# Loading four operand blocks straight into the place of their low parts, and splitting two of them later in the list

## The chip, the cores and the metric

The kernel runs on one core of a Trainium2 chip. The metric is the device time of one execution in microseconds (us), and less is better. TensorE (PE in the profile) multiplies matrices, with its weight loads shown as PEld; VectorE (DVE) and ScalarE (ACT) do the elementwise work; GpSimd (POOL) and SyncE (SP) mostly issue DMAs here. The rows of SP's DMA queue are marked SPq.

## The reference, cut to what matters

```python
xn = layernorm(x)                                  # x: 1 x 2048 x 640
a = einsum("bsd,ed->bse", xn, dft_hid_re)          # transform along the hidden dimension
b = einsum("bsd,ed->bse", xn, dft_hid_im)
y = einsum("ts,bse->bte", dft_seq_re, a) - einsum("ts,bse->bte", dft_seq_im, b)
gate, up = xn @ W_gate, xn @ W_up                  # 640 x 1728 each
h = (gate * (gate > 0)) * up
return x + y + h @ W_down                          # 1728 x 640
```

Everything is float32, 2048 tokens by 640 channels. Two branches read the same normalised tokens: a Fourier mixing and a gated network.

## The kernel before, in words

**Arithmetic.** A float32 operand is split into a high part, which ScalarE rounds by a copy (L125), and a low part, the source minus the high part, which VectorE makes (L126). `split(hi, lo, src)` issues these two instructions. `mm3` (L128) then runs three matmuls, high by high, high by low and low by high (L131 to L133), of 128 by 128 weights on 512 columns. Matrix products are cut in two in each direction and computed by seven block products in place of eight, which is why the code is full of blocks B11, B12, B21, B22 and of sums T1 to T4 of them.

**Phases.** The first phase normalises the tokens and multiplies them, as weights, with the columns of the sequence transform, streamed from `in_dft` in four chunks of 512 columns. In a chunk every transform block (T10, T11, ... T43 in the list of names) is one unit: a DMA of 128x1024 floats (L690) into a `raw` or `tk` buffer, a sum on VectorE (L686), a split into a `cb` buffer of a ring of three (L722, L723), and 12 or 18 matmuls. The name's first two characters say which of the products, the last digit says which of four groups of tokens. The second phase (`gate_up`, L881) runs over 13 tiles of 128 of the 1728 inner channels, for each half of the tokens. Its operands are the nine blocks of a **set**: the normalised tokens, transposed, as B11, B12, B21, B22, X4 and T1 to T4, 128x1024 floats each. The third phase (`project`, L1094) multiplies the results by the output matrices.

**The first set.** GpSimd's DMAs write its blocks to DRAM during the first phase (L416, L448), from buffers of the pool `stage`, which holds two tiles of 128x1024 floats. During the last chunk of the first phase they come back: `load_set` (L752) gets a `stage` tile for a block, loads the block into it (L760, on SP), and later splits it from there (L764) into the high and low places that `set_parts` (L741) gives. T2, T1, T3 and T4 have their places in a tile `sets_b`, in memory that held the layernorm's tiles (the profile calls it `r`, as digits are left out of names). B11, B21, X4, B12 and B22 have theirs in `xs_early`, the memory of the first half of the tokens, so they can be split only when the last matmuls on that part of the tokens are done. The same two `stage` tiles serve afterwards for the weights of the 64 channels that are left over (L940) and for two loads that the third phase will want (L1041, L1042).

**Order.** `phase` (L789) turns a list of names into units; `drive` (L768) goes through them and issues, at step i, the preparation (sums and splits) of unit i-2, the loads of unit i, and the matmuls of unit i-4. A `K` in the list loads one of T2, T1, T3, T4 (in this order), an `A` loads one of B11, B21, X4, B12, B22, and an `s` splits the block that has waited longest. This gives the program order. It is not the order on the engines: a planner at build time goes by its own costs, takes what is ready on an engine, and prefers what stands earlier in the program. So a load or split that stands late in the list can be put much earlier, into a place where the engine has nothing better. Within one engine, the order it chose is then fixed, and an instruction that waits holds up all behind it. In the second phase the order on PE, DVE and ACT is written by hand (L1072), that of SP and GpSimd is the planner's.

**The passage to the second phase.** The order written by hand begins with the weights of the left-over channels: `rest_weights` splits them (L942), 30 matmuls use them (`gate_up_rest`, L944), and in their shade the first tile's weights are loaded (L845) and split in two halves (L861, L865), with sums in between (L851 to L855). Then comes `gate_up(0)`: the first blocks it takes are B11, B21 and X4, then T1, T2, T4, X4, B22 and T3.

The list of the last chunk before is:

```python
phase(NCHUNK - 1, "T10 T11 T12 T13 T20 K B220 T21 s K B221 T22 s K T23 B222 s K B223 T30 s A T31 A T32 s A T33 s A T40 s A T41 s T42 s T43")
```

Of the kernel before, what the change touches and what calls it, by code (L numbers as in the profile page):

```python
# [7 lines left out]
F32 = mybir.dt.float32  # L8
# [10 lines left out]
NCHUNK = S // CH  # L19
# [40 lines left out]
def fnet_reglu_kernel(  # L60
# [63 lines left out]
    def split(hi, lo, src):  # L124
        nc.scalar.activation(hi, src, AF.Copy)  # L125
        return nc.vector.tensor_tensor(lo, src, hi.bitcast(F32), op=OP.subtract)  # L126
# [342 lines left out]
    def sums_124(g):  # L469


        def make():
            both = lambda g, cs: [xn_block(g, cs, v) for v in range(2)]
            a11, a21, a12, a22 = both(g, K1), both(g, K2), both(g + NH, K1), both(g + NH, K2)
            s1, s2 = (i.rearrange("p (j d) -> p j d", j=SG) for i in (lambda t: (t[:, :CH], t[:, CH:]))(stage()))
            w = s4_part(g)
            tt = nc.vector.tensor_tensor
            f = lambda i: i.bitcast(F32)
            tc.keep_in_program_order(tt(s1, f(a21[0]), f(a22[0]), op=OP.add))
            tt(s1, s1, f(a22[1]), op=OP.add)  # L480
            tt(s2, s1, f(a11[0]), op=OP.subtract)
            tt(s2, s2, f(a11[1]), op=OP.subtract)
            split(*a21, s1)

            tt(s1, f(a12[0]), s2, op=OP.subtract)
            tt(s1, s1, f(a12[1]), op=OP.add)
            split(*a11, s2)
            split(w[:, :, 0], w[:, :, 1], s1)

        todo.append((idle, make, idle, idle))  # L490

    def sums_3(g):


        def make():
            s = stage()[:, :CH].rearrange("p (j d) -> p j d", j=SG)
            tt = nc.vector.tensor_tensor
            a22, s2 = ([xn_block(n, cs, v).bitcast(F32) for v in range(2)] for n, cs in ((g + NH, K2), (g, K1)))
            tc.keep_in_program_order(tt(s, a22[0], s2[0], op=OP.subtract))
            tt(s, s, a22[1], op=OP.add)  # L500
            tt(s, s, s2[1], op=OP.subtract)
            split(xn_block(g + NH, K1, 0), xn_block(g + NH, K1, 1), s)

        todo.append((idle, make, idle, idle))
# [236 lines left out]
    def set_parts(q, i):  # L741
        if i in SETS_A:
            t, b = xs_early, (SETS_A_NEXT, SETS_A)[q].index(i) * 2 * W2
        else:
            t, b = late["sets_b"][q], SETS_B.index(i) * 2 * W2
        return t[:, b : b + W2], t[:, b + W2 : b + 2 * W2]
# [3 lines left out]
        return h[:, j * CH : (j + 1) * CH], l[:, j * CH : (j + 1) * CH]  # L750

    def load_set(q, blocks, get=stage):  # L752
        t = {}

        def load():
            if "sets_b" not in late:
                late["sets_b"] = {1: get_r1(F32R)}
            for i in blocks:
                t[i] = get()
                nc.sync.dma_start(t[i], sets[q][i])  # L760

        def prepare():
            for i in blocks:
                split(*set_parts(q, i), t[i])  # L764

        return load, prepare, idle, idle
# [17 lines left out]
    early_sets, first_sets = list(SETS_A), list(SETS_B)  # L784
# [4 lines left out]
    def phase(c, names):  # L789


        for n in names.split():
            if n == "K":
                later = load_set(1, [first_sets.pop(0)])
                todo.append((later[0], idle, idle, idle))
                splits.append((idle, later[1], idle, idle))
            elif n == "A":
                later = load_set(1, [early_sets.pop(0)])
                todo.append((later[0], idle, idle, idle))
                splits.append((idle, later[1], idle, idle))  # L800
            elif n == "s":
                todo.append(splits.pop(0))
            elif n[0] == "W":
                sums_124(int(n[1]))
            elif n[0] == "V":
                sums_3(int(n[1]))
            elif n[0] == "B" and n[2] == "1":
                first_stream(int(n[3]), n[:3], int(n[4]))
            else:
                stream(c, n[:-1], int(n[-1]))  # L810
            if steps and len(todo) >= SET_UNITS[-len(steps)]:
                token_sets(*steps.pop(0))

    for n in ("B11", "B21"):
        for g in range(NH):
            phase(0, f"{n}0{g} {n}1{g}")
    phase(0, "B1120 B1130 B1121 B1131 W0 B1122 B1132 B1123 W1 B1133 B2120 B2130 W2 B2121 B2131 B2122 V0 W3 B2132 B2123 B2133")
    phase(0, "V1 T10 T11 V2 T12 T13 V3 T20 B220 T21 B221 T22 T23 B222 B223 T30 T31 T32 T33 T40 T41 T42 T43")
    for c in range(1, NCHUNK - 1):
        phase(c, "T10 T11 T12 T13 T20 B220 T21 B221 T22 T23 B222 B223 T30 T31 T32 T33 T40 T41 T42 T43")  # L820
    assert not steps, len(steps)
    phase(NCHUNK - 1, "T10 T11 T12 T13 T20 K B220 T21 s K B221 T22 s K T23 B222 s K B223 T30 s A T31 A T32 s A T33 s A T40 s A T41 s T42 s T43")
    assert not early_sets and not first_sets
    drive(4, 2)
    ph1.close()
# [158 lines left out]
    def next_set(i, n, since=1, get=stage3, soon=False):  # L984

        load, prepare, _, _ = load_set(0, [i], get)

        def first():
            if 0 not in late["sets_b"] and i in SETS_B:
                late["sets_b"][0] = pool("sets").tile([P, len(SETS_B) * 2 * W2], F32R, name="sets_b")  # L990
            load()

        loads[n - since].append(first)
        (urgent if soon else besides)[n].append(prepare)
# [342 lines left out]
```

## Time and profile before

| what | value |
|---|---|
| time, median of 3 runs (range) | 1027.43 us (1026.66 to 1028.2) |
| the profiled execution's own time | 1026.78 us |
| its span, first to last instruction | 1025.0 us |
| mean granted TensorE clock | 0.999 |
| PE busy | 1019.8 us, 4525 matmuls |
| DVE busy | 818.4 us |
| ACT busy | 443.9 us |
| DMA | 236.45 MB, mean 231 GB/s |

The profiled execution lies 0.65 us below the median, inside the range of the three runs. Its own time is 1.78 us above its span. Times inside the trace are counted from the span's start. A row of the timeline gives start, duration, engine, line, operation, tile written and tiles read; in brackets stands how long the engine had stood idle before it, and for whom. The windows give, for stretches of the span, each engine's busy time and its number of instructions. The rows of the waits give the total, the number and the longest.

### The profile page before, as it was taken

To read this page: it belongs to the slowest core of one execution; us is meant where nothing else is said; L and a number is where in the kernel's file an instruction comes from. 1 tells how busy PE (TensorE), PEld (TensorE's weight loads), DVE (VectorE), ACT (ScalarE), POOL (GpSimd) and SP (SyncE) were. 2 spreads that over 40 slices of the span, in tenths; PEclk is the share of its full clock that TensorE was granted. 3 is DMA by queue.
4 is the path that set the end of the run, shared out by engine and by line. 5 is a ranking of instruction groups with operands and counts; after the bars stand their busy time and mean duration, and the time that the engine had idled before them with its cause. 6 is when DMAs were issued, how large, how long until landed. Compare 5 with 4: busy or idle time off the path is not lost.

```text
span 1025.0 us, 12537 instructions
## 1 busy us (share of the span) xinstructions
PE 1019.8 (99%) x4525; PEld 844.5 (82%) x4525; DVE 818.4 (80%) x1113; ACT 443.9 (43%) x571; POOL 96.9 (9%) x161
## 2 busy tenths in 40 slices
PE   9999999999999999999999999999999999999998
PEld 8888888888888888888888888888888888888886
DVE  7967977979989797688878988887586779787776
ACT  6664453333334443333335444443454434553442
POOL 2000010122110001421110000000000001000000
PEclk9999999999999999999999999999999999999999
DMA  8884744966859745873474666654595747994654
GB/s 329 320 284 156 265 152 137 341 245 211 353 195 359 254 169 174 260 239 134 175 249 151 212 239 232 216 219 173 192 354 190 254 147 232 379 334 155 216 172 160
DMA packets 104542, 236.45 MB, mean 231 GB/s; under 512 B 11936, under 2 KB 55328, under 8 KB 102944
## 3 DMA queue, kind: packets, MB, share of 16 engines
q1 hardware_dynamic: 86896, 165.49, 47.6%
q0 software_dynamic: 17152, 69.74, 18.4%
q8 instruction: 35, 0.57, 0.2%
q10 hardware_dynamic: 432, 0.43, 0.1%
q14 instruction: 27, 0.22, 0.1%
HBM read 179.50 MB, written 55.07 MB: 229 GB/s over the span
## 4 chain that ended last, share of the span: by engine, by line
PE 99%; DVE 0%; issue 0%
PE ps L132 32%; PE ps L131 32%; PE ps L133 32%; PE ps L519 3%; PE ps L548 1%; PE ps L1221 1%; PE ps L113 1%; DVE y L1252 0%; DVE warm L109 0%; DVE eps_t L102 0%; DVE half_t L104 0%
## 5 line engine op out<-in xcount | busy, mean ns | idle before, releaser
L133 PE MATMUL ps<-cb,wt 128*128 128x512 f32 x412 | 159.9, 388 | 0.0
L132 PE MATMUL ps<-cb,wt 128*128 128x512 f32 x412 | 159.9, 388 | 0.0
L131 PE MATMUL ps<-cb,wt 128*128 128x512 f32 x412 | 159.9, 388 | 0.0
L126 DVE TENSOR_TENSOR cb<-rw,cb 128x1024 fp32r<-128x1024 f32 x83 | 93.9, 1132 | 51.6 <-ACT cb L125 51.3
L125 ACT ACTIVATE cb<-rw 128x1024 fp32r<-128x1024 f32 x83 | 81.9, 987 | 117.5 <-PE ps L133 103.0
L125 ACT ACTIVATE cb<-raw 128x1024 fp32r<-128x1024 f32 x64 | 67.9, 1061 | 102.5 <-PE ps L133 91.6
L131 PE MATMUL ps<-xs_early,gw 128*128 128x512 f32 x260 | 101.2, 389 | 0.0
L133 PE MATMUL ps<-xs_early,gw 128*128 128x512 f32 x260 | 101.2, 389 | 0.0
L132 PE MATMUL ps<-xs_early,gw 128*128 128x512 f32 x260 | 101.2, 389 | 0.0
L126 DVE TENSOR_TENSOR cb<-raw,cb 128x1024 fp32r<-128x1024 f32 x64 | 78.2, 1221 | 28.7 <-ACT cb L125 28.3
L122 ACT ACTIVATE gw<-z 128x1024 fp32r<-128x1024 f32 (+1 forms) x52 | 57.7, 1110 | 79.7 <-DVE z L855 74.1
L131 PEld LDWEIGHTS ps<-cb,wt 128*128 128x128 f32 x412 | 77.3, 188 | 16.0
L132 PEld LDWEIGHTS ps<-cb,wt 128*128 128x128 f32 x412 | 77.3, 188 | 16.0
L133 PEld LDWEIGHTS ps<-cb,wt 128*128 128x128 f32 x412 | 77.3, 188 | 15.9
L131 PE MATMUL ps<-cb,xs_late 128*128 128x512 f32 x232 | 90.3, 389 | 0.0
L132 PE MATMUL ps<-cb,xs_late 128*128 128x512 f32 x232 | 90.3, 389 | 0.0
L133 PE MATMUL ps<-cb,xs_late 128*128 128x512 f32 x232 | 90.3, 389 | 0.0
L131 PE MATMUL ps<-cb,xs_early 128*128 128x512 f32 x226 | 87.9, 389 | 0.0
L133 PE MATMUL ps<-cb,xs_early 128*128 128x512 f32 x226 | 87.9, 389 | 0.0
L132 PE MATMUL ps<-cb,xs_early 128*128 128x512 f32 x226 | 87.9, 389 | 0.0
L122 ACT ACTIVATE u<-ps 128x512 f32<-128x512 f32 x52 | 31.0, 597 | 91.5 <-PE ps L133 91.5
L865 DVE TENSOR_TENSOR gw<-z,gw 128x1024 fp32r<-128x1024 f32 (+1 forms) x52 | 64.6, 1282 | 2.2 <-ACT gw L122 2.2
(198 smaller groups left out, 1970.8 us busy)
## 6 DMA issues: line engine op xcount, KB each, us to landing
raw<-in_dft SPq DMA_DIRECT2D x94, 512.0 KB, 5.5
wt<-wparts SPq DMA_DIRECT2D x70, 256.0 KB, 3.1
z<-in_wgu SPq DMA_DIRECT2D x26, 640.0 KB, 3.9
hd<-ob POOLq DMA_DIRECT2D x26, 512.0 KB, 3.8
wparts<-pw POOLq DMA_DIRECT2D x12, 1024.0 KB, 4.1
rw<-hd SPq DMA_DIRECT2D x24, 512.0 KB, 6.2
tk<-in_dft SPq DMA_DIRECT2D x16, 512.0 KB, 8.0
rw<-pq SPq DMA_DIRECT2D x16, 512.0 KB, 6.3
```

What stands on the lines that cost most here:

```text
L113: nc.tensor.matmul(ps[:, :P], warm, warm, start=True, stop=True)
L122: return nc.scalar.activation(o, i, AF.Copy)
L125: nc.scalar.activation(hi, src, AF.Copy)
L126: return nc.vector.tensor_tensor(lo, src, hi.bitcast(F32), op=OP.subtract)
L131: nc.tensor.matmul(ps, wh, mh, start=first, stop=False, skip_group_check=more)
L132: nc.tensor.matmul(ps, wh, ml, start=False, stop=False, skip_group_check=more)
L133: nc.tensor.matmul(ps, wl, mh, start=False, stop=last, skip_group_check=more)
L519: nc.tensor.matmul(E[0, key], xn_part(n * SG + j, d)[v == 1], b[:, int(v == 2), j], start=False, stop=n % NH == NH - 1 and (j, v) == (SG - ...
L548: nc.tensor.matmul(E[c, key], xn_part(j, d)[v == 1], b[c][0][:, int(v == 2), j], start=j == 0 and v == 0, stop=False)
L865: tt(self.w[:, 1, cs], self.z[:, cs], self.w[:, 0, cs].bitcast(F32), op=OP.subtract)
L1221: nc.tensor.matmul(B[out], w[:, v, oo : oo + P], b, start=False, stop=u == len(units) - 1 and v == 1, skip_group_check=more)
```

## The change

`load_set` may be called with no place to get. Then a block is loaded into the low place that `set_parts` gives it, and the split runs in place: ScalarE copies the high part out of the low place, and VectorE subtracts in place. T2, T1, T3 and T4, all the blocks called `K`, are loaded so. The list of the last chunk changes too: T2 and T1 keep about their places, the five `A` blocks are loaded and split some units earlier, and the loads of T3 and T4 move behind T40 and T41, with their splits behind T43, the last transform block. The number of instructions of each kind, of bytes moved and of matmuls stays as it was.

```diff
     def load_set(q, blocks, get=stage):
...
             for i in blocks:
-                t[i] = get()
+                t[i] = get() if get else set_parts(q, i)[1].bitcast(F32)
                 nc.sync.dma_start(t[i], sets[q][i])
...
             if n == "K":
-                later = load_set(1, [first_sets.pop(0)])
+                later = load_set(1, [first_sets.pop(0)], None)
...
-    phase(NCHUNK - 1, "T10 T11 T12 T13 T20 K B220 T21 s K B221 T22 s K T23 B222 s K B223 T30 s A T31 A T32 s A T33 s A T40 s A T41 s T42 s T43")
+    phase(NCHUNK - 1, "T10 T11 T12 T13 T20 K B220 T21 K s B221 T22 T23 s A B222 A B223 s T30 A s T31 T32 A s T33 A s T40 K T41 s K T42 T43 s s")
```

## The prediction, on record before the result

> **What bounds the kernel now.** I read the page first, then the waits of PE and the two ends of the timeline.
>
> ```profile
> span 1025.0 us, 12537 instructions
> ...
> PE 1019.8 (99%) x4525; PEld 844.5 (82%) x4525; DVE 818.4 (80%) x1113; ACT 443.9 (43%) x571; POOL 96.9 (9%) x161
> ...
> PEclk9999999999999999999999999999999999999999
> ...
> PE 99%; DVE 0%; issue 0%
> ```
> ```profile
> PE ps L113 <- DVE warm L109: 1.1, 1, 1.1
> ```
> ```profile
> 1020.58 0.28 PE L133 MATMUL ps<-cb,wt 128*128 128x256 f32 x1
> ...
> 1020.89 0.42 DVE L1252 TENSOR_TENSOR y<-ps,y 128x256 f32<-128x256 f32 x1 [0.29 <-PE ps L133]
> ```
>
> TensorE bounds it, everywhere. Its only recorded wait is the 1.1 us before the first matmul; the last ends at 1020.58 + 0.28 = 1020.86. Between lie 1020.86 - 1.1 = 1019.8 us, exactly its busy time, at full clock. So there is **nothing to win**: the change takes no matmul away, and outside the matmuls only 1025.0 - 1019.8 = 5.2 us are left, at the two ends, which it does not touch. A gain above 0.2% (2.05 us, about what a measurement of this kernel can tell from no change) has no place to come from. The question is whether the change makes TensorE wait, so I look at how much room its suppliers have in the last chunk.
>
> ```profile
> 309.97:320.85 10.88, 10.88 (x50) 9.01 (x49) 10.18 (x11) 6.26 (x6) 1.10 (x2) 1.00 1.00 384
> 320.85:331.73 10.88, 10.88 (x50) 9.01 (x49) 10.76 (x12) 4.14 (x4) 0.54 (x1) 1.00 0.97 348
> 331.73:342.60 10.87, 10.87 (x49) 9.01 (x48) 10.09 (x11) 5.19 (x5) 1.07 (x2) 1.00 0.98 376
> 342.60:352.13 9.53, 9.53 (x44) 7.88 (x43) 6.62 (x7) 3.80 (x5) 0.00 (x0) 1.00 0.62 202
> 352.13:363.01 10.88, 10.88 (x50) 9.01 (x49) 7.97 (x7) 5.55 (x6) 0.00 (x0) 1.00 0.43 138
> ```
>
> After the stretch the columns are its length, the busy time of PE, PEld, DVE, ACT, POOL, the granted clock, the DMA share and GB/s. From 310 to 342 VectorE idles for only 0.70 + 0.12 + 0.78 = 1.6 us and the DMA engines are full. From 342 on both have room: VectorE idles 2.91 us in each of the next two rows. **The risk stands at 310 to 342.**
>
> **The change part by part.**
>
> *Stage waits removed.* These are the loads of the blocks and what SP waited for:
>
> ```profile
> 306.81 0.80 SPq L760 DMA_DIRECT2D st<-set  x2
> ...
> 316.97 0.33 SPq L760 DMA_DIRECT2D st<-set  x1
> ...
> 332.45 0.61 SPq L760 DMA_DIRECT2D st<-set  x1
> ...
> 340.08 4.66 SPq L760 DMA_DIRECT2D st<-set  x2
> ```
> ```profile
> SPq L760 <- DVE xs_early L126: 12.5, 3, 5.9
> ...
> SPq L760 <- DVE r L126: 6.5, 3, 3.9
> ...
> SPq L760 <- DMA set<-st: 3.1, 1, 3.1
> ```
>
> T2 and T1 were loaded at 306.81, as soon as the set had reached DRAM (the 3.1 us), T3 at 316.97, T4 at 332.45, B11 and B21 from 340.08 on. Each of the later four stood behind a `stage` tile: SP waited 6.5 us for the low parts of `r`. With the change none of these four needs to wait: T3 and T4 have their own place, and B11 and B21 get the two `stage` tiles. SP wins 6.5 us, and the dft loads queued behind it come earlier, worth nothing while TensorE never idles. X4, B12 and B22 still wait for the low parts in `xs_early` (12.5 us), as their `stage` tiles still come free only then; that stays.
>
> *Loads moved.* Although T3 and T4 now stand late in the list, a load in the planner's hand goes out when its place is free, as T2's did: its place in the list is behind T20, whose matmuls end at 352.13, and it was loaded at 306.81. So I expect up to six loads from 306.8 on in place of two: four more blocks of 128x1024x4 = 524 KB, each 524/384 = 1.37 us of the DMA engines at the 384 GB/s of the first row above. The bytes by 345 us are the same; for some 10 us the dft loads come up to 4 x 1.37 = 5.5 us later.
>
> *Splits moved.* Four high and four low parts are made as before, only at other times.
>
> ```profile
> L125 ACT ACTIVATE r<-st x4: 1061/1062/1063, 310.2 to 338.8; 128x1024 fp32r<-128x1024 f32 x4
> L126 DVE TENSOR_TENSOR r<-st,r x4: 1216/1219/1219, 315.7 to 343.1; 128x1024 fp32r<-128x1024 f32 x4
> ...
>   DMA st<-set: 7.7, 3
> ```
>
> An in-place split is not in the trace. The nearest row is L686, VectorE writing over one of its sources:
>
> ```profile
> 318.00 1.22 DVE L686 TENSOR_TENSOR raw<-raw,tk 128x1024 f32<-128x1024 f32 x1
> 319.13 1.22 DVE L126 TENSOR_TENSOR cb<-raw,cb 128x1024 fp32r<-128x1024 f32 x1
> 320.27 1.22 DVE L686 TENSOR_TENSOR raw<-raw,tk 128x1024 f32<-128x1024 f32 x1
> ```
>
> It takes 1.22 us (1.14 from start to start), like the low part from a `stage` tile, 1.219; I take the same, cost **0**, and no gain is possible there, since the elements are the same.
>
> The low parts could now fall into the full stretch. VectorE's gaps there took T2, T1 and T3 (315.7 to 338.8); T4's came at 343.1. If all four fall before 342, that is one more, 1.14 us, against 1.6 us of idle time: **0**, and 0.5 us to spare. The lows in `xs_early` stay tied to the matmuls on that memory, whatever the list says: 0.
>
> *What the burst costs.* The rows around it, ScalarE's first:
>
> ```profile
> 307.49 1.06 ACT L125 ACTIVATE cb<-raw 128x1024 fp32r<-128x1024 f32 x1 [3.02 <-PE ps L133]
> 310.20 2.27 ACT L125 ACTIVATE r<-st 128x1024 fp32r<-128x1024 f32 x2 [1.65 <-DMA st<-set]
> 312.37 1.04 ACT L125 ACTIVATE cb<-raw 128x1024 fp32r<-128x1024 f32 x1
> 314.29 1.06 ACT L125 ACTIVATE cb<-raw 128x1024 fp32r<-128x1024 f32 x1 [0.88 <-ACT cb L125]
> ```
> ```profile
> 338.80 1.06 ACT L125 ACTIVATE r<-st 128x1024 fp32r<-128x1024 f32 x1 [4.41 <-DMA st<-set]
> ```
> ```profile
> 328.56 1.22 DVE L126 TENSOR_TENSOR cb<-raw,cb 128x1024 fp32r<-128x1024 f32 x1
> ```
> ```profile
> 330.37 0.39 PE L131 MATMUL ps<-cb,xs_late 128*128 128x512 f32 x1
> ```
>
> ScalarE waited 7.7 us in all for blocks that had not landed, once 4.41 us: the planner takes loads to be faster than they are in the full stretch, and the transform blocks' high parts stand behind. That cost nothing then. After the change the third block of the burst would land at 310.2 + 2 x 1.37 = 312.9, the fifth at 315.7, the sixth at 317.1. Likeliest the `cb` at 312.37 goes ahead of T3 (it comes earlier in the list), T3 follows at 315.7 at worst, and the next `cb` starts at 316.7, not 314.29; its low part comes at 317.8, not 316.86, and VectorE idles for 0.95 us. The tightest place behind is chunk 2's T43: its low ends at 328.56 + 1.22 = 329.78, its first matmul is at 330.37, room 0.59. So TensorE waits 0.95 - 0.59 = 0.36, say **0.4 us**. The bounds are 0 and 3.5 us (the first rival).
>
> [...]
>
> *The sum.* 1026.78 + 0.4 = 1027.2 against the profiled execution; the median lies 0.65 above it, so **1027.8 us**.
>
> **The rivals.**
>
> *ScalarE stands behind the burst (slower).* If T3 and T4 are put ahead of the `cb` at 312.37, that `cb` (chunk 2's T32) waits for the last landing. Units of 12 matmuls take 12 x 0.227 = 2.72 us; five of them before 330.37, at 316.77, T32's matmuls begin. With four T blocks in the burst T4 lands at 314.3, its high part, 0.97 from start to start, makes the `cb` start at 315.3; adding 1.06 and 1.22 for its two parts gives 317.6, so TensorE waits 0.8 us. With six in it: 317.1, then 318.1, then 320.4, **3.5 us**, and VectorE has no idle time to catch up. For it speaks the 4.41 us wait; against it, that T32 ranks higher and its `raw` is there long before. It decides from a landing after 315.5 (above 2.05 us). The time is 1028.2 to 1031.0, likeliest 1030.2.
>
> *The clock falls.* No row here shows a stall of TensorE long enough to lower its clock. If 3.5 us did, half clock for as long again would cost 1.7 us more: 1032.7. The Trainium skill (TensorE: Matmul & The Clock Gate, Part 1) has such a rule: after about 3.4 us idle the clock halves, until a busy window of that length. By it the first rival at its far end would turn into this one.
>
> *The splits really stand behind T43.* Then they delay the passage to the second phase:
>
> ```profile
> 393.58 0.83 DVE L126 TENSOR_TENSOR wr<-st,wr 128x640 fp32r<-128x640 f32 x1 [0.81 <-ACT wr L125]
> ```
> ```profile
> 394.43 0.38 SPq L1042 DMA_DIRECT2D st<-in_hid  x1
> 394.90 3.98 SPq L845 DMA_DIRECT2D z<-in_wgu  x2
> ```
> ```profile
> 400.24 1.23 DVE L865 TENSOR_TENSOR gw<-z,gw 128x1024 fp32r<-128x1024 f32 x1 [0.98 <-ACT gw L122]
> ...
> 404.37 1.36 DVE L865 TENSOR_TENSOR gw<-z,gw 128x1152 fp32r<-128x1152 f32 x1 [1.23 <-ACT gw L122]
> ```
> ```profile
> 405.17 0.39 PE L131 MATMUL ps<-xs_early,gw 128*128 128x512 f32 x1
> ...
> 408.57 0.39 PE L131 MATMUL ps<-r,gw 128*128 128x512 f32 x1
> ```
>
> Two more low parts ahead of L942's put it 2.27 us later, and L1042, which waits for its tile, and the weights behind L1042 on SP, and the whole chain to L865. The first L865 would end at 401.47 + 2.27 = 403.74, ahead of 405.17; the second at 405.73 + 2.27 = 408.00, ahead of 408.57. Room 0.57: the price is 0, and each us beyond costs one. Time 1027.4; slower only from 2.6 us on.
>
> *The change does nothing.* If the planner puts all in the old order, 1027.4.
>
> **How the numbers follow.** Chances: forecast 0.45 and 1026.6 to 1028.8 for it alone; the burst 0.33, of which a part (0.8 to 2 us) stays within 0.2%; the clock 0.05; the splits behind T43 0.07; no effect 0.07; a gain that I do not see 0.03. Slower by over 0.2%: 0.28 from the burst, 0.05 from the clock, 0.03 from the rest: 0.36. Within 0.2%: 0.61. The range reaches from the lowest time that no effect would show, 1026.4, to the burst's far end with some spread, 1031.6.
>
> **What would show it.** Right, if TensorE's busy time stays within 1 us of first-to-last matmul, all loads of `r` stand between 306 and 312, the `xs_early` rows keep their times, and PE's waits show no second row above 1 us. The burst would show as `ACT r <- DMA` waits above 4 us near 312 and a PE wait for `cb` between 316 and 331; the clock as a PEclk digit of 8 or less; the late splits as `r` rows of VectorE near 393. I am wrong if TensorE waits anywhere else, above all near 352 to 371, where the `xs_early` splits are.

## The result, and the profile after

| | before | after |
|---|---|---|
| time, median of 21 runs each (range) | 1027.43 us (1026.66 to 1028.65) | 1029.26 us (1028.16 to 1032.59) |
| ratio, 95% interval | | 1.0019 (1.0013 to 1.0025) |
| span of the profiled execution | 1025.0 us | 1026.8 us |
| mean granted TensorE clock | 0.999 | 0.999 |

The change made the kernel slower by 1.83 us, a ratio clear of no change and about as large as the 0.2% that separates "same" from "slower" in the prediction. The page of the kernel after, in the lines that answer to those shown of before:

```profile
span 1026.8 us, 12540 instructions
...
PE 1020.6 (99%) x4525; PEld 843.4 (82%) x4525; DVE 818.7 (80%) x1113; ACT 443.6 (43%) x571; POOL 96.9 (9%) x161
...
PEclk9999999999999999999999999999999999999999
```

The same matmuls, the same clock, and VectorE and ScalarE as busy as they were. The waits of PE have two rows that were not there:

```profile
PE ps L113 <- DVE warm L109: 1.1, 1, 1.1
PE ps L548 <- ACT xs_early L250: 0.5, 1, 0.5
PE ps L132 <- DVE cb L126: 0.4, 1, 0.4
```

The L548 row belongs to the first matmuls, at 6 us, far ahead of the change; such rows come and go from profile to profile (0.2 us in one experiment below, 0.6 in another, none in most). The last row is the change's. It counts less than is lost: a wait of a weight load stands in the rows of PEld (1.7 us in all, in the same place), part of it under the matmul before. A sharper reading is to set the starts of the same matmul in the two traces side by side. Counted from 0, matmul 47 begins 0.03 us earlier than before, the last 1.80 us later. From matmul 1427 to 1477, chunk 2's T33 to T43, the lag grows by **1.29 us** (0.24 to 1.53). The rest is 0.2 us within the first 18 us, 0.19 at 959 us and smaller pieces; profiles of kernels below that lost nothing show steps of this size at both places. These are the timeline's rows of the first and the largest step:

```profile
319.72 0.39 PE L131 MATMUL ps<-cb,xs_late 128*128 128x512 f32 x1
320.53 0.50 PE L132 MATMUL ps<-cb,xs_late 128*128 128x512 f32 x1 [0.42 <-DVE cb L126]
```

L131 needs only the high part and starts on time; L132 needs the low part and starts 0.81 us after it in place of 0.23. The low part it waits for, T33's, was made 2.4 us later than before. VectorE's row for it, of before and then of after:

```profile
316.86 1.22 DVE L126 TENSOR_TENSOR cb<-raw,cb 128x1024 fp32r<-128x1024 f32 x1
```
```profile
319.25 1.23 DVE L126 TENSOR_TENSOR cb<-raw,cb 128x1024 fp32r<-128x1024 f32 x1 [0.24 <-ACT cb L125]
```

VectorE was late since ScalarE was. SP's queue, then ScalarE, after:

```profile
301.27 0.33 SPq L761 DMA_DIRECT2D st<-set  x1
301.70 1.93 SPq L690 DMA_DIRECT2D raw<-in_dft  x2
309.91 0.33 SPq L761 DMA_DIRECT2D r<-set  x1
310.32 0.38 SPq L690 DMA_DIRECT2D raw<-in_dft  x1
310.76 0.42 SPq L761 DMA_DIRECT2D r<-set  x1
311.27 0.38 SPq L690 DMA_DIRECT2D raw<-in_dft  x1
311.82 0.73 SPq L761 DMA_DIRECT2D st<-set  x1
```
```profile
307.73 1.06 ACT L125 ACTIVATE cb<-raw 128x1024 fp32r<-128x1024 f32 x1 [3.02 <-PE ps L133]
313.47 1.06 ACT L125 ACTIVATE r<-r 128x1024 fp32r<-128x1024 f32 x1 [4.68 <-DMA r<-set]
314.44 1.04 ACT L125 ACTIVATE cb<-raw 128x1024 fp32r<-128x1024 f32 x1
317.20 1.06 ACT L125 ACTIVATE r<-r 128x1024 fp32r<-128x1024 f32 x1 [1.73 <-DMA r<-set]
318.17 2.94 ACT L125 ACTIVATE cb<-raw 128x1024 fp32r<-128x1024 f32 x3
```

Before, T2 and T1 left SP together at 306.81. Now B11 goes out first, at 301.27 (it has a free `stage` tile, and its data were written by the first of the last two set DMAs, issued at 297.89), T2 only at 309.91 and T1 at 310.76. ScalarE stands idle for 4.68 us in front of T2 and 1.73 us in front of T1, and behind each stands a transform block that was not late: T32's high part at 314.44, not 312.37, and T33's at 318.17, not 314.29. VectorE waits 2.53 us for T32's:

```profile
315.51 1.23 DVE L126 TENSOR_TENSOR cb<-raw,cb 128x1024 fp32r<-128x1024 f32 x1 [2.53 <-ACT cb L125]
```

T2 could not leave because the DMA that writes the T blocks, GpSimd's L448, had not landed. It was issued at nearly the same time (301.16 before, 301.39 after), and landed after 5.5 us before and after 8.5 us now, at 301.39 + 8.5 = 309.9, when T2 leaves. The DMA's rows for 300 to 312, of before and then of after:

```profile
set<-st POOLq DMA_DIRECT2D x1, 512.0 KB, 5.5
```
```profile
set<-st POOLq DMA_DIRECT2D x1, 512.0 KB, 8.5
```

T3 and T4 did not join a burst. SP issued them at 332.36 and 335.77, near where T4's load stood before. ScalarE stood idle for 2.8 us in front of each, and it cost nothing: the lag is 1.55 us at matmul 1500 and at matmul 2000.

### The profile page after: what moved, and what is told of

The parts are those of the page before. It is cut to its first block, busy times and chain, and to the rows that moved or that the text cites. A ratio compares the mean times of both kernels' runs of the same rounds, so it can differ in the third digit from the quotient of the medians.

```text
span 1026.8 us, 12540 instructions
## 1 busy us (share of the span) xinstructions
PE 1020.6 (99%) x4525; PEld 843.4 (82%) x4525; DVE 818.7 (80%) x1113; ACT 443.6 (43%) x571; POOL 96.9 (9%) x161
## 4 chain that ended last, share of the span: by engine, by line
PE 97%; DVE 1%; DMA 1%; ACT 0%; issue 0%; ACTq 0%
PE ps L133 31%; PE ps L132 31%; PE ps L131 31%; PE ps L519 3%; DMA raw<-in_dft 1%; PE ps L1222 1%; DVE cb L126 0%; DVE raw L686 0%; DVE sb L561 0%; DVE sa L558 0%; DVE r L126 0%; DVE cb L631 0%; DVE tk L686 0%; DVE xs_early L331 0%; ACT r L328 0%
## 5 line engine op out<-in xcount | busy, mean ns | idle before, releaser
L131 PE MATMUL ps<-cb,wt 128*128 128x512 f32 x412 | 159.9, 388 | 0.0
L132 PE MATMUL ps<-cb,wt 128*128 128x512 f32 x412 | 159.9, 388 | 0.0
L131 PE MATMUL ps<-xs_early,gw 128*128 128x512 f32 x260 | 101.2, 389 | 0.0
L132 PE MATMUL ps<-xs_early,gw 128*128 128x512 f32 x260 | 101.1, 389 | 0.0
L132 PE MATMUL ps<-cb,xs_late 128*128 128x512 f32 x232 | 90.6, 391 | 0.5 <-DVE cb L126 0.4
L131 PEld LDWEIGHTS ps<-cb,wt 128*128 128x128 f32 x412 | 77.3, 188 | 16.4 <-issue 0.3
L132 PEld LDWEIGHTS ps<-cb,wt 128*128 128x128 f32 x412 | 77.3, 188 | 15.9
L131 PE MATMUL ps<-cb,xs_late 128*128 128x512 f32 x232 | 90.2, 389 | 0.0
L132 PE MATMUL ps<-cb,xs_early 128*128 128x512 f32 x226 | 87.9, 389 | 0.0
L131 PE MATMUL ps<-cb,xs_early 128*128 128x512 f32 x226 | 87.9, 389 | 0.0
```

The costliest lines, as they stand in the source:

```text
L131: nc.tensor.matmul(ps, wh, mh, start=first, stop=False, skip_group_check=more)
L132: nc.tensor.matmul(ps, wh, ml, start=False, stop=False, skip_group_check=more)
```

## The experiments

The **theory**: a `stage` tile comes free, B11's load goes out ahead of the DMA that writes T1 to T4, so T2 and T1 come late, and ScalarE, which takes its instructions in order, holds up transform blocks behind them. **Rivals**: the new list, with its later splits, does it; the split in place is slower; the DMA engines are full, so that the dft loads come late whatever ScalarE does; it is B21's load that makes T1 late. `tc.issue_after(x)` puts an instruction behind the instruction x in its engine's order. Each kernel was timed beside the kernel before on its chip: the first four beside 1027.44 us, the last four beside 1026.98 us.

**The places alone, with the list of before.**

```diff
-    phase(NCHUNK - 1, "... T20 K B220 T21 K s B221 T22 T23 s A B222 A B223 s T30 A s ...")
+    phase(NCHUNK - 1, "... T20 K B220 T21 s K B221 T22 s K T23 B222 s K B223 T30 s A ...")
```

> The list of before, with T2, T1, T3 and T4 loaded into their low places. Theory (ScalarE behind late loads): the two stage tiles are free, so B11 still goes out ahead of T2, the DMA that writes the set lands near 310 instead of 307, T2 and T1 land some 3 and 6 us later than before, and the high parts of the transform blocks behind them on ScalarE are late: TensorE waits 1 to 2 us in all between 316 and 333, time 1028.6 to 1029.8. Rival 1 (the new list does it, by its later and earlier splits): no wait there, 1027.4 +- 0.4. Rival 2 (the in-place split is slower): VectorE's rows on r longer than 1.22 us, and 1027.4 to 1029, by how much longer they are.

Measured: 1031.03 us, ratio 1.0033 (1.0021 to 1.0046). More was lost than theory said, 3.6 us by the starts of the same matmuls, T33 to T43, and ScalarE's rows show why:

```profile
313.80 1.06 ACT L125 ACTIVATE r<-r 128x1024 fp32r<-128x1024 f32 x1 [4.85 <-DMA r<-set]
314.77 1.04 ACT L125 ACTIVATE cb<-raw 128x1024 fp32r<-128x1024 f32 x1
317.60 1.06 ACT L125 ACTIVATE r<-r 128x1024 fp32r<-128x1024 f32 x1 [1.79 <-DMA r<-set]
318.57 1.04 ACT L125 ACTIVATE cb<-raw 128x1024 fp32r<-128x1024 f32 x1
321.98 1.06 ACT L125 ACTIVATE r<-r 128x1024 fp32r<-128x1024 f32 x1 [2.37 <-DMA r<-set]
```

With T3 early in the list, its load stands where B21's stood after, and a third late block stops ScalarE at 319.6. So the places do the harm, and the new list about halves it; that it does so by taking T3 out of the way is put to the test below, with B21 held. Rival 2 falls too: VectorE's splits in place took what they took from `stage`.

```profile
L126 DVE TENSOR_TENSOR r<-r x4: 1216/1216/1218, 318.1 to 346.9; 128x1024 fp32r<-128x1024 f32 x4
```

**The list alone, with all blocks through `stage`.**

```diff
-                later = load_set(1, [first_sets.pop(0)], None)
+                later = load_set(1, [first_sets.pop(0)])
```

> The list of after, with all blocks loaded through a stage tile. Theory: T2 and T1 take the two stage tiles at once, B11 can't go ahead of them, ScalarE's rows at 310 to 315 are those of before, and TensorE waits for nothing: 1027.4 +- 0.4. Rival 1 (the new list): 1028.6 to 1029.8, with a wait of TensorE somewhere behind 310.

Measured: 1027.35 us, ratio 0.9997 (0.9988 to 1.0005). T2 and T1 left together at 307.52, and TensorE's only wait is the 1.1 us at the start. The list by itself does nothing that could be measured. ScalarE's rows were not quite those of before: the set DMA took 6.0 us, and T32's high part came at 313.44, 1.07 us later than before, which cost nothing.

**The A blocks held behind T2 and T1.**

```diff
-                nc.sync.dma_start(t[i], sets[q][i])
+                if q == 1 and i in SETS_A:
+                    with tc.issue_after(late["k"]):
+                        nc.sync.dma_start(t[i], sets[q][i])
+                else:
+                    d = nc.sync.dma_start(t[i], sets[q][i])
+                    if i in (T2, T1):
+                        late["k"] = d.ins
```

> After, with the loads of B11, B21, X4, B12 and B22 held behind the loads of T2 and T1 on SP. Theory: the DMA that writes the set lands near 307 again, T2 and T1 leave together near 306.8, ScalarE's waits for them fall from 6.4 us to 2 us or less, and TensorE's waits between 316 and 333 go: 1027.4 to 1027.9. Rival 3 (the DMA engines are full, so the dft loads behind the blocks come late whichever goes first): T2 and T1 leave early, but VectorE still waits for raw tiles and TensorE loses 1 us or more: 1028.5 to 1029.5.

Measured: 1027.22 us, ratio 1.0000 (0.9991 to 1.0008). T2 and T1 leave first, and ScalarE hardly waits for them:

```profile
305.77 0.80 SPq L765 DMA_DIRECT2D r<-set  x2
306.67 0.38 SPq L690 DMA_DIRECT2D raw<-in_dft  x1
307.29 0.32 SPq L763 DMA_DIRECT2D st<-set  x1
```
```profile
309.55 1.06 ACT L125 ACTIVATE r<-r 128x1024 fp32r<-128x1024 f32 x1 [1.11 <-DMA r<-set]
310.77 1.06 ACT L125 ACTIVATE r<-r 128x1024 fp32r<-128x1024 f32 x1 [0.16 <-DMA r<-set]
311.74 1.04 ACT L125 ACTIVATE cb<-raw 128x1024 fp32r<-128x1024 f32 x1
```

All of the loss goes with the new places and the new list still there. The set DMA landed after 4.7 us.

**The high parts of T2 and T1 held on ScalarE, the loads left late.**

```diff
...
+                h = nc.scalar.activation(flat(b, 0), src, AF.Copy)
+                if (c, name, g) == (NCHUNK - 1, "T1", 3):
+                    late["high"] = h.ins
...
-                split(*set_parts(q, i), t[i])
+                if q == 1 and i in (T2, T1):
+                    with tc.issue_after(late["high"]):      # the high part of T13, last chunk
+                        split(*set_parts(q, i), t[i])
+                else:
+                    split(*set_parts(q, i), t[i])
```

> After, with the high parts of T2 and T1 held on ScalarE behind that of T13 of the last chunk (near 340); the loads stay as late as in after. Theory: nothing stands behind a late block on ScalarE any more, the high parts of chunk 2's T32 and T33 start within 0.5 us of before (312.4 and 314.3), and TensorE's waits between 316 and 333 go though T2 still leaves near 309.9: 1027.4 to 1028.0. Rival 3 (the dft loads themselves come late): the waits stay at 1 us or more, 1028.5 to 1029.5. Four low parts then fall into 338 to 352, where VectorE idled 3 us before; if that is too many, a wait of up to 1 us shows at T13 to T21 instead.

Measured: 1026.89 us, ratio 0.9995 (0.9986 to 1.0003). SP still issued B11 at 301.04, T2 at 310.05 and T1 at 310.90, as late as after, and yet the transform blocks' high parts run evenly, waiting for nothing but their ring tile:

```profile
307.48 1.06 ACT L723 ACTIVATE cb<-raw 128x1024 fp32r<-128x1024 f32 x1 [3.02 <-PE ps L133]
311.56 1.06 ACT L723 ACTIVATE cb<-raw 128x1024 fp32r<-128x1024 f32 x1 [3.02 <-PE ps L133]
314.28 1.06 ACT L723 ACTIVATE cb<-raw 128x1024 fp32r<-128x1024 f32 x1 [1.66 <-PE ps L133]
```

The late loads alone cost nothing: VectorE waited 1.6 us for one raw tile and 0.3 us for a `tk` tile, and TensorE for none. The loss needs the splits of T2 and T1 ahead of the transform blocks. This run does not say on which engine: a low part follows its high part, so the two low parts left the stretch too (all rows of `r` on VectorE now start at 340.8 or later), and VectorE had 2.3 us less to do there.

That ScalarE passes the delay on is read from the kernels that kept these low parts. Between 310 and 330 VectorE stands idle 0.70 us before and 1.51 us with the list alone, without loss; 2.77 us after, 2.85 with T2 loaded twice, 5.03 with the places alone and 5.91 with B21 held, and each time it waits for a high part that ScalarE makes at or behind a late block, never for a DMA. Between matmuls 1426 and 1477 these four lose 1.29, 1.47, 3.6 and 4.5 us: what VectorE idles beyond some 1.4 to 1.5 us, TensorE loses.

**B11 alone held behind T2 and T1**, by the same edit as above with `(q, i) == (1, B11)` in place of `q == 1 and i in SETS_A`.

> After, with the load of B11 alone held behind the loads of T2 and T1 on SP. Theory (B11's load goes ahead of the DMA that writes the set, so that T2 and T1 are late, and ScalarE stands behind them): that DMA lands near 306 again, ScalarE's waits for T2 and T1 are 2 us or less in all, TensorE waits for nothing behind 310: 1027.0 to 1027.9. Rival (B21's load and the others behind T1 make the burst): 1028.3 or more, with ScalarE's wait for T1 still 1.5 us or more.

Measured: 1026.73 us, ratio 0.9996 (0.9987 to 1.0004). The set DMA landed after 5.0 us, T2 and T1 left at 306.36, ScalarE waited 1.00 and 0.64 us for them. Both low parts stayed in the stretch (VectorE made them at 315.76 and 321.44, before at 315.73 and 321.40). The one load that jumped ahead is enough to explain all of the loss.

**B21 alone held**, behind the loads for T13 of the last chunk:

```diff
...
-                nc.sync.dma_start(t[i], sets[q][i])
+                if (q, i) == (1, B21):
+                    with tc.issue_after(late["raw"]):       # the last dft load of T13, last chunk
+                        nc.sync.dma_start(t[i], sets[q][i])
+                else:
+                    nc.sync.dma_start(t[i], sets[q][i])
```

> After, with the load of B21 alone held on SP behind the loads for T13 of the last chunk (near 324); B11 still goes first, and T3 takes B21's place on SP near 312. Theory: T2 and T1 are as late as in after, and T3 is a third late block for ScalarE to stand behind, so the loss is that of the run with the places alone: 1030.3 to 1031.5, with TensorE's waits between 316 and 335 some 3 to 4 us. Rival (B21's load makes T1 late): ScalarE's wait for T1 falls below 1 us and the time to 1028.5 or less.

Measured: 1031.20 us, ratio 1.0038 (1.0025 to 1.0051), as theory said; by the matmuls' starts 4.5 us are lost, a little more than the 3 to 4 expected. T3 went out at 311.22 in B21's place, and ScalarE stood idle 4.37, 3.56 and 1.98 us in front of T2, T1 and T3. The wait for T1 did not shrink; the rival falls.

**The places alone, with the high parts of T2, T1 and T3 held** as in the run above.

> The list of before with the new places (1031.03 before), and the high parts of T2, T1 and T3 held on ScalarE behind that of T13 of the last chunk. Theory: all of the 3.6 us go, though the blocks land as late as they did: 1026.9 to 1028.0, no wait of TensorE between 316 and 335. Rival (part of the 3.6 us are the dft loads, late behind the blocks): 1028.5 to 1030, with VectorE waiting for raw or tk tiles for 1 us or more.

Measured: 1026.82 us, ratio 0.9998 (0.9989 to 1.0006), with a wait of TensorE only at the start. All of the 3.6 us go, though T2, T1 and T3 leave SP as late as they did (310.19, 311.04 and 311.99). VectorE did wait for dft loads, 1.5 us for a raw tile and 0.6 us for a `tk` tile, without loss. As above, the low parts left the stretch with the high parts.

**Before, with T2 loaded twice.**

```diff
                 nc.sync.dma_start(t[i], sets[q][i])
+                if (q, i) == (1, T2):
+                    nc.sync.dma_start(t[i], sets[q][i])
```

> Before, with T2 loaded twice into its stage tile; the second load waits until the first has landed, and SP with it, so that T2 is ready some 4 us later than before (near 314), with nothing else of the change. Theory: a late block on ScalarE is enough, and the high part of the transform block behind it is late; one late block in place of two costs less than after: TensorE waits 0.3 to 1.3 us between 316 and 333, 1027.7 to 1028.7. Rival (it takes the new places or the new list as well): no wait, 1027.4 +- 0.4.

Measured: 1028.57 us, ratio 1.0016 (1.0007 to 1.0024). A loss of this kind comes in the kernel before too, with nothing of the change in it but one more load of 512 KB and SP's wait for it:

```profile
315.31 1.06 ACT L125 ACTIVATE r<-st 128x1024 fp32r<-128x1024 f32 x1 [1.83 <-DMA st<-set]
316.28 2.00 ACT L125 ACTIVATE cb<-raw 128x1024 fp32r<-128x1024 f32 x2
319.59 1.06 ACT L125 ACTIVATE cb<-raw 128x1024 fp32r<-128x1024 f32 x1 [1.32 <-issue]
324.40 1.06 ACT L125 ACTIVATE r<-st 128x1024 fp32r<-128x1024 f32 x1 [3.75 <-DMA st<-set]
325.37 1.04 ACT L125 ACTIVATE cb<-raw 128x1024 fp32r<-128x1024 f32 x1
```
```profile
PE ps L132 <- DVE cb L126: 1.1, 1, 1.1
```

The place is not quite where I expected it: the late T2 at 315.31 was borne, and of the 1.47 us that the matmuls' starts lose 1.35 fall at T43 (matmuls 1476 and 1477), behind a block that ScalarE waited 3.75 us for, until 324.40. That block is T3: its load stands in the same place of SP's order as before, left 0.69 us later (317.66) and landed 1.96 us later.

No version beats the kernel before: the five without the loss, the list alone among them, all have 1 in their interval, as they must where TensorE never idles.

## Why the prediction was right, and where its steps were off

- **What bounds the kernel, and that nothing can be won**: held. Five kernels, from 1026.73 to 1027.35 us, came back to the time of before and none went below it by a measurable amount.
- **Where the risk stands, 310 to 342**: held; the change's 1.29 us lie between 320 and 333.
- **The split in place, cost 0**: held. 1220 ns after, against 1219 from `stage`.
- **The stage waits removed, 6.5 us of SP**: these waits are gone, and the 12.5 us for `xs_early` stayed, as forecast. But between 295 and 345 SP waited 14.7 us for the set DMAs, where it had waited 3.1:

```profile
SPq L761 <- DMA set<-st: 14.7, 2, 8.5
```

- **The mechanism of the loss**: held: ScalarE in order behind a block that has not landed, then VectorE, then TensorE. It is shown by the rows of after and by the hold of B11; the holds of the high parts moved low parts as well. The forecast and its first rival shared it, and differed by what stands behind which block.
- **What the burst costs, 0.4 us: mis-sized.** It measured 1.29 us. The step that failed is *Loads moved*: I let T2 and T1 leave at 306.8 as before, and put four more loads behind them. In truth one of these, B11, went ahead. I had noted that SP waited 3.1 us for the set's DMA before T2 left, but not that the B blocks' DMA was issued 3.5 us before the T blocks' (297.66 and 301.16 in the trace of before), so that with a free `stage` tile B11 is ready first. Its load and the two dft loads behind it then ran while the T blocks' DMA was on its way, which took 8.5 us in place of 5.5. T2 was late by 3.1 us at its issue already, where my working had it leave and land on time. T33's high part came at 318.17, where I had 316.7 at worst, and T32's, which I took to be safe, at 314.44. The room of 0.59 us was misread too: T43's low part is needed only by its second matmul, L132, which starts at 330.59 in the trace of before, so the room was 330.59 - 329.78 = 0.81. And the largest step came at T33, not at T43, which I had taken for the tightest place.
- **T3 and T4 between 306 and 312**: wrong. They left at 332.36 and 335.77. A free place does not bring a load out at once: the place in the list counted, since with the same places and the list of before T3 left at 311.84. How the planner weighs the two is not shown. It was T3's lateness that kept the loss down: with T3 early the matmuls lost 3.6 us in place of 1.29.
- **The splits really behind T43**: did not happen. All four rows of `r` on VectorE lie between 317.8 and 345.3.
- **The clock**: stayed at full speed (0.999 granted). The longest step between the starts of two matmuls is 0.81 us there, and 1.47 us in any run (T2 loaded twice: 1.24 us of waiting and the 0.23 us of the matmul). The rule of the Trainium skill (TensorE: Matmul & The Clock Gate, Part 1) on idle times of some 3.4 us was never tested by any run here.
- **The time, 1027.8, and the range to 1031.6**: 1029.26 lies between the forecast and the first rival's likeliest 1030.2, inside the rival's own 1028.2 to 1031.0. It is outside the 1026.6 to 1028.8 that the forecast gave for itself alone. What was written as the less likely branch of one mechanism was nearer to what happened, and the signs say so too: ScalarE's wait of 4.68 us for T2 and TensorE's wait for `cb` at 320.53 are those named for the burst, while "all loads of `r` between 306 and 312", named for the forecast, failed. That the total fell well inside the range was partly luck: T2 and T1 came later than I worked out, T3 and T4 were not in the way, and the two errors pull in opposite directions.

## What to carry to other kernels

When a buffer is freed, ask which load will take it first, and what that load then overtakes: here the harm came not from the blocks that got new places but from a block that got their old one. On an engine that takes its instructions in order, a filler that depends on a DMA is not free because the engine has idle time; it is only as harmless as its data are punctual, and it should stand behind the work that feeds the bounding engine until they are surely there. Where the bounding engine never idles, a change in its suppliers can only lose, and the loss has to be looked for in the stretch where they have the least to spare. There the idle time of the nearest supplier, less what it idles without loss, was a good measure of it here.

## What the runs showed of the hardware that was not expected

The 512 KB DMA that writes the T blocks from GpSimd's queue took 4.7 to 6.0 us to land with two dft loads of SP beside it (before, the list alone, hold of the A blocks, hold of B11, T2 twice), and 8.2 to 9.1 us where a third load of 512 KB had been issued 0.1 us before it (after, the places alone, hold of B21, the high parts held in both runs). One more load of the same size thus cost it some 3 us, about twice the 1.37 us that its bytes take at 384 GB/s. Why it is twice is not settled: no run varied the size of that load, or its moment other than by holding it until the DMA had landed.
